# Decode attention with a token mixer: one 8 KB-row piece of the output weights loaded in five parts, x and a small bias through another queue

## The chip, the cores and the metric

The kernel runs on one core of a Trainium2 chip. The metric is the device time of one execution in microseconds (us): 1286.22 us is the median of three runs before the change (1286.08 to 1286.46). All data are float32.

## The reference, cut to what matters

One decode step over 8 sequences, with 32 query heads that share 8 key and value heads of 8192 cached positions, beside a token-mixing MLP:

```python
xn = layernorm(x)                                   # x: 8 x 1 x 512
# attention on layernorm'd xn
q  = (xn @ wq)                                      # 512 x 4096, 32 heads of 128
s  = einsum("bhqd,bhkd->bhqk", q, repeat(k_cache, 4)) * 128**-0.5
o  = einsum("bhqk,bhkd->bhqd", softmax(s), repeat(v_cache, 4))
A  = o.reshape(8, 1, 4096) @ wo                     # wo: 4096 x 512
# mixer over the token axis (one token, 1792 hidden units)
h  = layernorm(xn)
Bm = einsum("bdf,fs->bds", gelu(einsum("bsd,sf->bdf", h, w1) + b1), w2) + b2
out = x + A + transpose(Bm)
```

Each of the two caches holds 8 x 8 x 8192 x 128 numbers, 268 MB; wq and wo hold 8.4 MB each. Everything else is small.

## The kernel before, in words

The work is cut into 32 steps ("pairs"): one sequence and two of its key/value heads, whose keys (8.4 MB) and values (8.4 MB) lie in memory as 128 rows of 64 KB, one row for each partition. They go into a ring of five slots of 4 MB (`raw`). The loads of wq, of keys and values and of wo are all issued by the SyncE sequencer (SP in the profile, one queue, called q1 there), in the order in which the code calls `load` and `load_wo`; an issue waits until the slot that it writes has been read. Each load of 128 rows is divided over the core's 16 DMA engines, 8 rows each, and an engine works off the loads in the order of issue.

For each pair VectorE transposes the keys in 32x32 blocks (`turn`), TensorE makes the scores (`scores`), ScalarE the exponentials (`exps`), TensorE transposes them (`send_on`) and multiplies the values (`values`). Beside it ScalarE and GpSimd work through the mixer (`mx_step`). A loop (`tc.For_i`) runs over pairs 2 to 29 in twos; pairs 0 and 1, and 30 and 31, are written out. The order on each engine is the order of the code.

At the start x (8 rows of 2 KB) and b2 (one number, read into 8 partitions) are loaded through ScalarE's own queue (q10), and w1, b1 and w2 through GpSimd's (q0, whose descriptors GpSimd writes by software). x goes through the layer norm (`layer_norm`) and is turned into `lend`, the stationary operand of the q projection (`q_project`).

At the end wo, seen as 128 rows of 32 chunks of 512 numbers, comes in two halves (`load_wo`). The first half is one load of 128 rows of 32 KB. The second is cut by the table `WO_HIGH = (8, 4, 2, 1, 1)` into five loads of 16, 8, 4, 2 and 2 KB for each row, so that the last products wait for little: chunks 16 to 23, 24 to 27, 28 and 29, 30, 31. The matmuls of line 512 use chunks 0 to 27 (`sums`), ScalarE copies their result (`folded`), and `y_add` (line 520) adds chunks 28 to 31 and the folded sum in `hb`. VectorE copies the result (line 527) and SP stores it (line 528).

The framework gives each load that SP or ScalarE issues one of eight completion semaphores in turn (DMAHW0 to DMAHW7 in the listings of instructions), and each that GpSimd issues one of another set (DMASW0 and on). A load that is given a semaphore which an earlier load still has to raise is issued only after that load has landed.

Of the kernel before, what the change touches and what calls it, by code (L numbers as in the profile page):

```python
# [14 lines left out]
B, D, HQ, HKV, SK, DH, F = 8, 512, 32, 8, 8192, 128, 1792  # L15
REP = HQ // HKV
P = 128
# [22 lines left out]
ROUNDS = (LAST + 1 - 2 * FIRST) // PER  # L40
GROUPS = N_PR // PER
WO_HIGH = (8, 4, 2, 1, 1)
MJ = NF // PER
MIX = (4, 4)
PAD = 96
# [6 lines left out]
def attn_mixer_kernel(ctx: ExitStack, tc: tile.TileContext, x, kc, vc, wq, wo, w1, b1, w2, b2, out):  # L52
    nc = tc.nc
# [10 lines left out]
    def slot(at, n=1):  # L64
        return slots[:, at:at + n, :]
# [12 lines left out]
    def misc():  # L78
        return ps_m.tile([P, 512], F32, name="misc")
# [7 lines left out]
    RES = one.tile([HALF, NWO, ROUNDS], F32, name="res")  # L87
    lend = one.tile([P, 2, P], F32, name="lend")
    x_sb = OB[:B, 0, :]
    nc.scalar.dma_start(x_sb, x.rearrange("b s d -> (b s) d"))  # L90
    b2t = const.tile([B, 1], F32, name="b2t")
    nc.scalar.dma_start(b2t, bass.AP(tensor=b2.tensor, offset=b2.offset, ap=[[0, B], [1, 1]]))
    body = slot(2, 2).rearrange("p s m -> p (s m)")
    rows = wq.rearrange("(p e) n -> p (e n)", p=P)
    for a in range(2):
# [41 lines left out]
    def load_wo(high):  # L137
        t = slot(3 if high else 0).rearrange("p s (c n) -> p (s c) n", n=D)
        rows = wo.rearrange("(p c) n -> p c n", p=P)
        at = 0  # L140
        for n in WO_HIGH if high else (NWO // 2,):
            o = high * NWO // 2 + at
            nc.sync.dma_start(t[:, at:at + n], rows[:, o:o + n])  # L143
            for c in range(n):
                WO[o + c] = t[:, at + c]
            at += n
# [29 lines left out]
    m = misc()  # L176
# [16 lines left out]
    rows = tmp[:, :2 * REP]  # L193
# [7 lines left out]
    for k in range(2):  # L201
        for a in range(NB):
            o = a * W + a // 2 * HW
# [3 lines left out]
    for c in range(NCH):  # L207
        for s in range(2):
            o = s * HW + c * REP
# [17 lines left out]
    nc.gpsimd.memset(acc, 0.0)  # L227
    tabs = const.tile([P, ROUNDS, 2, MJ + 1], F32, name="tabs")
    tabw = const.tile([P, ROUNDS, MJ + 1], F32, name="tabw")
    for k in range(PER):  # L230
        js = slice(k * MJ, (k + 1) * MJ)
        for t, src in ((tabs[:, k::PER, 0], w1t), (tabs[:, k::PER, 1], b1t), (tabw[:, k::PER], w2t)):
            n = len(range(k, ROUNDS, PER))
            nc.gpsimd.tensor_copy(t[:, :, :MJ], src[:, js].unsqueeze(1).to_broadcast([P, n, MJ]))
    for t, src in ((tabs[:, :, 0], w1t), (tabs[:, :, 1], b1t), (tabw, w2t)):
        nc.gpsimd.tensor_copy(t[:, :, MJ:], src.unsqueeze(2))
    nows = const.tile([P, 2, MJ + 1], F32, name="nows")
    noww = const.tile([P, MJ + 1], F32, name="noww")
# [4 lines left out]
    for k in range(2):  # L243
        t = const.tile([P, CH_T * W + W], F32, name=f"pt{k}")
# [216 lines left out]
    with tc.For_i(0, ROUNDS, 1, iteration_sync=SYNC) as r:  # L461
        for k in range(PER):
            n = FIRST + k
# [18 lines left out]
    n = LAST - 1  # L482
# [11 lines left out]
    n = LAST  # L494
    score_half(n, True)
    load(vc, n, 2, 0)
    score_half(n, False)
    load(vc, n, 1, 1)
    load_wo(0)
    softmax_and_values(n, lambda: load_wo(1))  # L500
    take(n - 1)
    total(HALF)
# [7 lines left out]
    for c in range(FOLD):  # L510
        o = c % NB * W
# [44 lines left out]
```

## Time and profile before

| | |
|---|---|
| median of the runs | 1286.22 us (1286.08 to 1286.46) |
| the profiled execution | 1286.04 us |
| its span, first to last instruction | 1284.2 us |
| granted TensorE clock | 0.805 |
| TensorE busy | 767.5 us (60% of the span) |
| VectorE busy | 696.9 us (54%) |
| GpSimd / ScalarE busy | 248.1 us (19%) / 228.8 us (18%) |
| read from memory | 553.69 MB, 431 GB/s over the span |
| SP's DMA queue | 99.6% of the 16 DMA engines' time |

A row of a table by windows gives, for each stretch of the span, the busy time of each engine with its number of instructions, the granted clock, the share of the 16 DMA engines' time that packets took, and what they moved; a packet is counted where it starts, so a short window can show a share over 1. A row on a DMA queue gives its packets, their megabytes and their share of the 16 engines' time. In a row of the timeline stand start, length, engine, line, operation, and in brackets how long the engine was idle before it and what ended that.

### The profile page before, as it was taken

The numbers are of one execution on the slowest core, as the hardware profiler recorded it, in microseconds if no ns is written. First come the engines' busy times: TensorE is split into PE (matmuls) and PEld (weight loads), VectorE is DVE, ScalarE is ACT, GpSimd is POOL, SyncE is SP. The second block draws the span as 40 slices with busy tenths as digits, with TensorE's granted clock in tenths as the row PEclk, the third lists the DMA queues.
The fourth block names the chain that finished last, engine by engine and source line by source line (L and its number), as shares of the span: only waits on it lengthen the run. The fifth ranks groups of instructions, "written<-read, shape, count | busy, mean of one in ns | idle before, by whom it ended". The sixth has DMA issues, their size and how long they took to land. (4 is left out here: it accounts for less than half of the span.)

```text
span 1284.2 us, 13214 instructions
## 1 busy us (share of the span) xinstructions
PE 767.5 (60%) x4830; PEld 170.9 (13%) x4830; DVE 696.9 (54%) x615; ACT 228.8 (18%) x382; POOL 248.1 (19%) x244
## 2 busy tenths in 40 slices
PE   4367556576465665556666475765656665464677
PEld 1111111111011111111111011110111110011112
DVE  3666644466654465644466554565644466543661
ACT  0000221212222121221212222121221211222000
POOL 1000221202222022221212222022221212222000
PEclk8788787887777897788787777877778887778888
DMA  9999999999999999999999999999999999999998
GB/s 409 425 442 425 448 427 433 445 429 433 425 447 429 431 447 427 433 433 439 431 429 447 427 433 445 429 433 427 445 431 429 447 427 433 439 433 431 430 431 354
DMA packets 10975, 553.86 MB, mean 431 GB/s; under 512 B 1324, under 2 KB 1356, under 8 KB 1748
## 3 DMA queue, kind: packets, MB, share of 16 engines
q1 hardware_dynamic: 10836, 553.67, 99.6%
q8 instruction: 8, 0.13, 0.0%
q10 hardware_dynamic: 32, 0.02, 0.0%
q0 software_dynamic: 96, 0.02, 0.0%
q14 instruction: 3, 0.02, 0.0%
HBM read 553.69 MB, written 0.02 MB: 431 GB/s over the span
## 5 line engine op out<-in xcount | busy, mean ns | idle before, releaser
L293 DVE STREAM_TRANSPOSE raw<-raw 128x2048 f32<-128x2048 f32 x256 | 565.4, 2275 | 232.8 <-DMA raw<-in_A_k_cache_dram 218.6
L302 PE MATMUL acc<-raw,z 128*32 128x512 f32 x2048 | 372.8, 815 | 433.9 <-DVE raw L293 385.7
L340 PE MATMUL acc<-raw,pt 128*32 128x512 f32 x2048 | 245.5, 621 | 10.9 <-DMA raw<-in_A_v_cache_dram 5.5
L399 POOL TENSOR_TENSOR g<-g,noww 128x512 f32<-128x512 f32 x98 | 101.8, 1039 | 376.2 <-ACT g L394 376.2
L302 PEld LDWEIGHTS acc<-raw,z 128*32 128x32 f32 x2048 | 47.0, 124 | 737.7 <-DVE raw L293 550.9
L322 ACT ACTIVATE t2k<-acc,ns 128x512 f32<-128x512 f32 x32 | 22.0, 687 | 603.2 <-PE acc L340 525.5
L394 ACT ACTIVATE g<-hb,nows 128x512 f32<-128x512 f32 x112 | 87.5, 782 | 192.8 <-POOL macc L400 175.4
L329 DVE STREAM_TRANSPOSE pt<-misc 128x512 f32<-128x512 f32 x64 | 45.9, 717 | 126.0 <-PE misc L328 121.6
L397 POOL TENSOR_TENSOR macc<-g,noww 128x512 f32<-128x512 f32 x14 | 14.5, 1038 | 515.8 <-ACT g L394 515.8
L400 POOL TENSOR_TENSOR macc<-macc,g 128x512 f32<-128x512 f32 x84 | 106.4, 1267 | 6.6
L340 PEld LDWEIGHTS acc<-raw,pt 128*32 128x32 f32 x2048 | 66.0, 114 | 174.7 <-issue 150.0
L316 DVE TENSOR_TENSOR t2k<-misc,hmask 128x128 f32<-128x128 f32 x32 | 9.3, 292 | 114.8 <-PE misc L314 114.8
L328 PE MATMUL misc<-t2k,send 128*128 128x512 f32 x128 | 65.1, 632 | 3.1 <-ACT t2k L322 3.1
L394 ACT ACT_TABLE_LOAD x28 | 35.9, 1283 | 94.5 <-PE hb L385 94.3
L309 DVE TENSOR_REDUCE mr<-acc 128x1 f32<-128x512 f32 x32 | 22.1, 690 | 52.9 <-PE acc L302 52.9
L409 ACT ACT_TABLE_LOAD x28 | 35.9, 1283 | 0.5
L347 ACT COPY ob<-acc 128x512 f32<-128x512 f32 x32 | 18.7, 585 | 74.3 <-PE acc L340 74.3
L328 PEld LDWEIGHTS misc<-t2k,send 128*128 128x128 f32 x128 | 22.0, 191 | 45.2 <-issue 41.9
L405 PE MATMUL misc<-macc,esel 128*8 128x512 f32 x30 | 15.3, 590 | 19.6 <-DVE esel L403 19.6
L385 PE MATMUL hb<-hn,hsel 8*128 8x512 f32 x28 | 18.9, 761 | 12.9 <-DVE hsel L384 12.9
L406 DVE TENSOR_TENSOR yrow<-misc,yrow 8x512 f32<-8x512 f32 x16 | 10.9, 679 | 19.2 <-PE misc L405 19.2
L262 PE MATMUL misc<-raw,lend 128*32 128x512 f32 x64 | 12.5, 953 | 11.3 <-DMA raw<-in_A_wq_dram 11.3
(99 smaller groups left out, 195.4 us busy)
## 6 DMA issues: line engine op xcount, KB each, us to landing
raw<-in_A_v_cache_dram SPq DMA_DIRECT2D x4, 4096.0 KB, 34.3
raw<-in_A_wq_dram SPq DMA_DIRECT2D x2, 4096.0 KB, 17.0
raw<-in_A_k_cache_dram SPq DMA_DIRECT2D x2, 4096.0 KB, 30.8
raw<-in_A_wo_dram SPq DMA_DIRECT2D x1, 4096.0 KB, 26.4
raw<-in_A_wo_dram SPq DMA_DIRECT2D x1, 2048.0 KB
raw<-in_A_wo_dram SPq DMA_DIRECT2D x1, 1024.0 KB, 29.9
raw<-in_A_wo_dram SPq DMA_DIRECT2D x1, 512.0 KB
raw<-in_A_wo_dram SPq DMA_DIRECT2D x2, 256.0 KB, 30.8
```

What stands on the lines that cost most here:

```text
L293: nc.vector.transpose(t, t)
L302: nc.tensor.matmul(SD[n][c * W:(c + 1) * W, :].rearrange("p (t j) -> p t j", j=W), Z[:, n % PER, q, (1 - k) * REP:(1 - k) * REP + W], t[:, ...
L309: nc.vector.tensor_reduce(mr, SD[n], AX.X, ALU.max)
L322: nc.scalar.activation(p, SD.pop(n), AF.Exp, bias=ns, scale=SCALE, accum_out=lr[:, n % PER:n % PER + 1])
L328: nc.tensor.matmul(m, send[:, k, :], p, start=True, stop=True)
L329: nc.vector.transpose(PT[k][:, :CH_T * W], m)
L340: d = nc.tensor.matmul(OD[n][j * W:(j + 1) * W, :].rearrange("p (c d) -> p c d", c=NCH), PT[k][:, t * W:(t + 1) * W], v[:, t], start=(not ...
L385: nc.tensor.matmul(hb, hsel.to_broadcast([B, P]), hn, start=True, stop=True)
L394: nc.scalar.activation(g, hb7 if last else hb, AF.Gelu_apprx_tanh, bias=nows[:, 1, j:j + 1], scale=nows[:, 0, j:j + 1])
L399: nc.gpsimd.tensor_tensor(g, g, w, op=ALU.mult)
L400: nc.gpsimd.tensor_add(acc7 if last else acc, acc7 if last else acc, g)
L409: nc.scalar.activation(small.tile([P, 1], F32, name="warm"), nil, AF.Exp)
```

## The change

Two edits. x and b2 are issued by GpSimd in place of ScalarE. And the piece of the second half of wo that starts at chunk 24 (four chunks, 8 KB for each of 128 rows) is loaded by five loads of 112, 5, 5, 5 and 1 rows in place of one. All of it stays on SP's queue and in the same place of the program; the bytes are the same.

```diff
 WO_HIGH = (8, 4, 2, 1, 1)
+TILT_AT, TILT = 24, (112, 5, 5, 5, 1)
...
-    nc.scalar.dma_start(x_sb, x.rearrange("b s d -> (b s) d"))
+    nc.gpsimd.dma_start(x_sb, x.rearrange("b s d -> (b s) d"))
     b2t = const.tile([B, 1], F32, name="b2t")
-    nc.scalar.dma_start(b2t, bass.AP(tensor=b2.tensor, offset=b2.offset, ap=[[0, B], [1, 1]]))
+    nc.gpsimd.dma_start(b2t, bass.AP(tensor=b2.tensor, offset=b2.offset, ap=[[0, B], [1, 1]]))
...
             o = high * NWO // 2 + at
-            nc.sync.dma_start(t[:, at:at + n], rows[:, o:o + n])
+            p = 0
+            for m in TILT if o == TILT_AT else (P,):
+                nc.sync.dma_start(t[p:p + m, at:at + n], rows[p:p + m, o:o + n])
+                p += m
```

Lines behind the first edit have other numbers after the change: 143 becomes 146, 512 becomes 516, 520 becomes 524, 528 becomes 532.

The two edits act on one another through the semaphores. SP's queue at the end of the program before, from the last two value loads on; "128x2048" is the piece of 8 KB rows, the brackets name what an issue waits for:

```order
L122 DMA raw<-in_A_v_cache_dram 128x8192 [waits DVE_49]
L122 DMA raw<-in_A_v_cache_dram 128x8192 [waits DMAHW3_49,DVE_49,PE_49]
L143 DMA raw<-in_A_wo_dram 128x8192 [waits DVE_49,PE_49]
L143 DMA raw<-in_A_wo_dram 128x4096 [waits DMAHW4_49,PE_49]
L143 DMA raw<-in_A_wo_dram 128x2048
L143 DMA raw<-in_A_wo_dram 128x1024
L143 DMA raw<-in_A_wo_dram 128x512 x2
L528 DMA out_dram<-g 4x8x128 [waits DMAHW5_49,DVE_49]
```

The same place after the change:

```order
L123 DMA raw<-in_A_v_cache_dram 128x8192 [waits DVE_49]
L123 DMA raw<-in_A_v_cache_dram 128x8192 [waits DMAHW1_49,DVE_49,PE_49]
L146 DMA raw<-in_A_wo_dram 128x8192 [waits DVE_49,PE_49]
L146 DMA raw<-in_A_wo_dram 128x4096 [waits DMAHW2_49,PE_49]
L146 DMA raw<-in_A_wo_dram 112x2048
L146 DMA raw<-in_A_wo_dram 5x2048 x3
L146 DMA raw<-in_A_wo_dram 1x2048 [waits DMAHW3_49]
L146 DMA raw<-in_A_wo_dram 128x1024 [waits DMAHW4_49]
L146 DMA raw<-in_A_wo_dram 128x512 [waits DMAHW5_49]
L146 DMA raw<-in_A_wo_dram 128x512 [waits DMAHW6_49]
L532 DMA out_dram<-g 4x8x128 [waits DMAHW7_49,DVE_49]
```

One load became five, and the four loads of wo behind the three small ones now wait for a semaphore that an earlier load raises: DMAHW3 and DMAHW4 belong to the two halves of the last values, DMAHW5 to the first half of wo, DMAHW6 to its 16 KB-row piece.

TensorE's last matmuls before the change (line 512 with `sums`, line 520 with `hb`):

```order
L512 MATMUL acc<-raw,ot 32x512 [waits DMAHW0_49]
L512 MATMUL acc<-raw,ot 32x512 x7
L512 MATMUL acc<-raw,ot 32x512 [waits DMAHW1_49]
L512 MATMUL acc<-raw,ot 32x512 x3
L520 MATMUL hb<-raw,ot 32x128 [waits DMAHW2_49]
```

And after it:

```order
L516 MATMUL acc<-raw,ot 32x512 [waits DMAHW6_49]
L516 MATMUL acc<-raw,ot 32x512 x7
L516 MATMUL acc<-raw,ot 32x512 [waits DMAHW3_49,DMAHW2_49,DMAHW7_49,DMAHW1_49,DMAHW0_49]
L516 MATMUL acc<-raw,ot 32x512 x3
L524 MATMUL hb<-raw,ot 32x128 [waits DMAHW4_49]
```

The order is the same; the matmul that begins chunk 24 waits for five loads in place of one.

GpSimd's queue at the start, before:

```order
L552 UNCONDITIONAL_BRANCH [waits barrier_Pool_Activation_PE_DVE_SP_gather]
masks.py:197 MEMSET ident 128x128
masks.py:199 ISA
masks.py:199 AFFINE_SELECT ident<-ident 128x128 [waits Pool_49]
L156 DMA pad<-in_B_w_dram 128x14
```

And after:

```order
L556 UNCONDITIONAL_BRANCH [waits barrier_Pool_Activation_PE_DVE_SP_gather]
L91 DMA ob<-in_A_x_dram 8x512
L93 DMA b2t<-in_B_b_dram 8x1
masks.py:197 MEMSET ident 128x128
masks.py:199 ISA
masks.py:199 AFFINE_SELECT ident<-ident 128x128 [waits Pool_49]
L160 DMA pad<-in_B_w_dram 128x14
```

The two small loads now stand ahead of the identity matrix and of the loads of w1, b1 and w2, and ScalarE's queue has none left.

## The prediction

> **What bounds the kernel now.** I read the page's slices and DMA rows first, then the end of the chain of waits, then the last microseconds by windows, then the start by the timeline. The page:
>
> ```profile
> DMA  9999999999999999999999999999999999999998
> DMA packets 10975, 553.86 MB, mean 431 GB/s; under 512 B 1324, under 2 KB 1356, under 8 KB 1748
> q1 hardware_dynamic: 10836, 553.67, 99.6%
> q10 hardware_dynamic: 32, 0.02, 0.0%
> ```
>
> The 16 DMA engines are busy in every slice and SP's queue has 99.6% of their time. No compute engine is over 60%. So only three things can move the time: when the engines start, what they lose underway, and how evenly they end. 431 GB/s over 16 engines is 26.9 GB/s each, so one row of 8 KB takes an engine 8192 B / 26.9 GB/s = 0.304 us.
>
> The page also shows how a load is spread. x and b2 are two loads of 8 rows and have 32 packets on q10: 2 x (8 data + 8 completions), so each went to eight engines, a row each. By that a load of 5 rows goes to five engines, one of 1 row to one, and 112 rows give each of 16 engines 7.
>
> The end of the chain of waits (start, length, what), and SP's store behind it:
>
> ```profile
> 1249.57 30.87 DMA raw<-in_A_wo_dram
> 1280.44 0.04 issue
> 1280.48 0.47 PE hb L520 x8
> 1280.98 0.29 DVE g L527
> ...
> 1281.30 0.71 SPq L528 DMA_DIRECT2D out_dram<-g  x1
> ```
>
> The last piece of wo lands at 1280.44; what follows is fixed. The windows before it:
>
> ```profile
> 1277.50:1278.00 0.50, 0.38 (x8) 0.03 (x4) 0.00 (x0) 0.00 (x0) 0.00 (x0) 1.00 1.02 410
> 1278.25:1278.50 0.25, 0.25 (x8) 0.00 (x0) 0.00 (x0) 0.00 (x0) 0.00 (x0) 1.00 0.81 320
> ...
> 1279.50:1279.75 0.25, 0.25 (x17) 0.10 (x5) 0.00 (x0) 0.19 (x1) 0.00 (x0) 1.00 0.57 221
> 1279.75:1280.00 0.25, 0.25 (x16) 0.25 (x14) 0.00 (x0) 0.00 (x0) 0.00 (x0) 1.00 0.29 107
> 1280.00:1280.25 0.25, 0.25 (x16) 0.12 (x6) 0.00 (x0) 0.00 (x0) 0.00 (x0) 1.00 0.02 8
> ```
>
> The column before the last is the DMA share. Until 1278 all work; from 1278.25 some are done (0.81); from 1279.50 the share is 0.57 = 9 of 16 engines; these nine end between 1279.75 and about 1280.15 (0.4 us). The other seven end up to 1.8 us earlier. If all ended together, the gain would be at most 7 x 1.8 / 16 = 0.8 us: the most that any tilt of rows can bring.
>
> Why nine are late: DMA rows of the windows 40 to 160, 1195 to 1198 and 1190 to 1285 (fetches of instructions), then the packets from 1181.3 to 1182, 1182.7 to 1183.4 and 1279.6 to 1280.2.
>
> ```profile
> q8 instruction: 4, 0.07, 0.2%
> ...
> q8 instruction: 1, 0.02, 1.8%
> ...
> q8 instruction: 4, 0.07, 0.2%
> ```
>
> ```profile
> DMA packets 22, 0.72 MB, mean 1030 GB/s; under 512 B 11, under 2 KB 11, under 8 KB 11
> ...
> DMA packets 8, 0.26 MB, mean 375 GB/s; under 512 B 4, under 2 KB 4, under 8 KB 4
> ...
> DMA packets 38, 0.06 MB, mean 99 GB/s; under 512 B 9, under 2 KB 9, under 8 KB 38
> ```
>
> A fetch holds one engine for 1.8% x 16 x 3 us = 0.9 us. Packets under 512 B are the completion marks, one for each engine and load. In the loop's last rounds 11 marks come together and four about 1.4 us later, after four fetches; after four more, nine are late at the end. So the late ones are engines that fetched instructions, one each, and one more.
>
> Which engines those are no view says. But in the packet list each packet starts where the one before it on its engine ended, so the 16 sequences can be followed through, apart from a few that coincide in the first 12 us. Eight of them carry x's rows, that is, an 8-row load's engines. Whichever way the coinciding ones are taken, at least four of those eight end among the nine late ones.
>
> **The change part by part.**
>
> *The rows.* Before, each engine has 8 rows of the piece. After: 7 for all, one more on five engines three times, and one on a single engine. If the small loads take the same engines each time, and the single row one of these: one engine 11 rows (+3 x 0.304 = +0.91 us), four 10 (+0.61), eleven 7 (-0.30). If a 5-row load's engines are among the eight that an 8-row load uses, of which at most four are early, then at least one loaded engine is late already; and five drawn from all 16 with nine late would be all early with a chance of (7x6x5x4x3)/(16x15x14x13x12) = 0.5%. If it has +0.91, the end moves by 0.91 less what that engine is ahead of the last, 0 to 0.4: +0.5 to +0.9. If only engines with +0.61 are late: +0.2 to +0.6. Had none been late, the last engine would gain 0.30. Bounds -0.30 and +0.91; I take +0.6, since with half of the eight late the odds are even for the one with eleven rows, and the latest counts.
>
> *TensorE.* Chunks 24 to 27 wait for the slowest of five loads, by the same sum +0.3 to +0.9 late:
>
> ```profile
> 1275.55 0.13 PEld L512 LDWEIGHTS acc<-raw,ot 128*32 128x32 f32 x4 [0.32 <-DMA raw<-in_A_wo_dram]
> 1277.97 0.16 PEld L512 LDWEIGHTS acc<-raw,ot 128*32 128x32 f32 x8 [1.03 <-DMA raw<-in_A_wo_dram]
> ...
> 1280.48 0.16 PEld L520 LDWEIGHTS hb<-raw,ot 128*32 128x32 f32 x8 [0.36 <-DMA raw<-in_A_wo_dram]
> ```
>
> The last wait (0.36 us of idle left) moves by as much as the first, so this costs 0; should chunk 24 slip more than the last piece, what exceeds 0.36 would come on top.
>
> *SP.* Four issues more, 2.31 / 5 = 0.46 us each, 1.8 us, and four new waits in a row. Behind the waiting sequencer stand only the pieces of 4, 2 and 2 KB and the store.
>
> ```profile
> 1247.70 2.31 SPq L143 DMA_DIRECT2D raw<-in_A_wo_dram  x5
> 1253.85 0.62 PE L340 MATMUL acc<-raw,pt 128*32 128x512 f32 x2
> 1261.14 5.12 PE L340 MATMUL acc<-raw,pt 128*32 128x512 f32 x32 [2.29 <-DMA raw<-in_A_v_cache_dram]
> 1270.80 8.24 PE L512 MATMUL acc<-raw,ot 128*32 128x512 f32 x56 [2.72 <-DMA raw<-in_A_wo_dram]
> 1282.30:1282.60 0.30, 0.00 (x0) 0.00 (x0) 0.00 (x0) 0.00 (x0) 0.00 (x0) 1.00 0.00 0
> 1282.60:1282.70 0.10, 0.00 (x0) 0.00 (x0) 0.00 (x0) 0.00 (x0) 0.00 (x0) 1.00 0.22 61
> ```
>
> The loads waited for have landed by 1253.85, 1261.1, 1270.8 and, for the last issue, 1275.55 (the 16 KB-row piece). From issue to first packet the store took 1282.6 - 1281.3 = 1.3 us, so the last piece is ready at about 1276.9. A late engine, with eight rows of 2 KB (8 x 0.076 = 0.6 us) left, wants it at 1279.5 or so; the earliest ones at about 1278.3 - 0.6 - 0.3 = 1277.4. Cost 0, with 0.5 us to spare there and over 2 us where it counts. Bounds: 0 and whatever the issue lags beyond 2.6 us.
>
> *x and b2.* Rows of the start, with the DMA row of the first 3 us and, for GpSimd's three loads, the time from issue to landing:
>
> ```profile
> q10 hardware_dynamic: 16, 0.02, 4.0%
> ...
> DMA to landing us min/median/max: 7.8/9.6/10.5
> 0.74 0.59 ACTq L90 DMA_DIRECT2D ob<-in_A_x_dram  x1
> 1.48 0.70 POOL L156 DMA_DIRECT2D pad<-in_B_w_dram  x1 [0.16 <-issue]
> 2.18 0.54 POOL L157 DMA_DIRECT2D pad<-in_B_b_dram  x1
> 2.69 0.68 DVE L163 BATCH_NORM_STATS2 st<-ob 8x6 f32<-8x512 f32 x1 [1.80 <-DMA ob<-in_A_x_dram]
> ...
> 5.46 0.19 DVE L179 COPY lend<-misc 128x32 f32<-128x32 f32 x1 [0.66 <-PE misc L178]
> 13.40 6.06 PE L262 MATMUL misc<-raw,lend 128*32 128x512 f32 x32 [7.98 <-DMA raw<-in_A_wq_dram]
> 22.80 6.47 PE L262 MATMUL misc<-raw,lend 128*32 128x512 f32 x32 [3.34 <-DMA raw<-in_A_wq_dram]
> 32.44 8.89 DVE L293 STREAM_TRANSPOSE raw<-raw 128x2048 f32<-128x2048 f32 x4 [17.87 <-DMA raw<-in_A_k_cache_dram]
> 43.92 0.52 POOL L418 MEMSET rep<- 128x512 f32 x1 [29.01 <-POOLq L461]
> ```
>
> GpSimd's loads took 7.8 to 10.5 us to land, so x lands at worst at 0.75 + 10.5 = 11.3, in place of 2.69. `lend` then is ready 2.96 us later, at 14.2, and the q projection starts 0.8 us late; its second half waits for wq until 22.80, with 3.34 us of idle before it: covered. VectorE's constants slip by up to 8.6 us into its 17.87 us of idle; GpSimd issues two more (1.25 us) into 29.01. Only if x came after 14 would SP's next key load be touched. For the DMA engines it is the same bytes: x's eight engines lose its share ahead of wq, 4.0% x 16 x 3 us / 8 = 0.24 us, and later serve them between wq's packets. Bounds -0.24 and +0.1; I take 0, since these engines are not behind at the end of it.
>
> Sum: 1286.04 + 0.6 = 1286.64 against the profiled execution. That lies 0.18 under the median, so 1286.8 for the runs.
>
> **The rivals.**
>
> 1. *The loaded engines are early ones:* -0.30, so 1285.9. For it: seven engines have 0.4 us or more to spare. Against: the count above, four late of eight; the fetches would have to fall on other engines after the change. 0.2.
> 2. *The change does not tilt:* 5 + 5 + 5 + 1 = 16, and if each small load took the next engines in turn, every engine would have 8 rows as before: 1286.2. No row shows whether two small loads share engines. 0.1. The Trainium skill's page DMA: Bandwidth & Descriptors, "Why a DMA increments its semaphore by 16 and not by 1", says that a load issued by SP uses the lowest-numbered engines; by that the rows pile up, as I took it.
> 3. *Engines get in each other's way:* in a load of 128 rows an engine always writes the same partitions; with 112 rows, 7 each, and rows 112 to 127 by other engines, their ways into memory may cross. Two that share a way would take 0.61 for a row; if that holds for half of an engine's 8 rows it is +1.2: 1287.4. For it: each engine runs at just the same rate now, which sharing would break. Against: no row shows sharing. 0.14. The skill's page SBUF — State Buffer, "Door 1: The DMA port swizzle", has such a rule: 16 ports, each for fixed groups of partitions, whose number reached sets the rate. By it the 112 rows don't divide evenly.
> 4. *The other side, slower beyond doubt:* SP's last wait becomes the bound. It decides once issue to first packet takes more than some 4 us in place of 1.3; for +2.6 us it must take 6.6: 1288.8. The queue's other first packets speak against it. 0.04.
>
> **How the numbers follow.** The forecast has 0.5, the rivals 0.2, 0.1, 0.14 and 0.04, something unseen 0.02. This kernel's time can be told from no change at about 0.2%, 2.6 us. Forecast and rivals 1 to 3 lie within it; rival 4 and a part of 3 don't: faster 0.02, same 0.92, slower 0.06. Range: from rival 1 with x's 0.24 (1285.7) to rival 3 (1287.4) with 0.3 on top, 1285.7 to 1287.7.
>
> **What would show it.** After the change, the share in the last windows should fall from 16 engines to nine as now, but one to five engines should end 0.3 to 0.9 us behind; the last wait of line 524 should end at about 1281.0. SP should issue wo in four bursts, the last at about 1275.6. The first layer norm should start at 6 to 11 us, and the q projection's second half still at 22.8. If the last wait ends at 1280.1 it is rival 1; if the piece of 8 KB rows takes clearly over 3 us, rival 3. Wrong altogether would be a gap in the DMA share at 1276 to 1279, or other engines fetching instructions.

## The result, and the profile after

The change costs 4.6 us: 1290.69 us (median of seven runs, 1289.29 to 1291.49) against 1286.08 (1285.69 to 1286.49) for the kernel before in the same call. The ratio is 1.0034 [1.0022, 1.0046]: slower by more than 0.2%, and outside the predicted range. The profiled execution took 1290.96 us with a span of 1289.2 us (before 1284.2), so 5.0 us are to be found in it.

The page and the DMA queues after the change:

```profile
DMA packets 11023, 553.86 MB, mean 430 GB/s; under 512 B 1372, under 2 KB 1404, under 8 KB 1796
q1 hardware_dynamic: 10852, 553.67, 99.5%
```

The bytes are those of before. SP's queue has 16 packets more (10836 before): the completion marks of 5 + 5 + 5 + 1 engines, so the small loads do go to five, five, five and one engine. DMA is still the bound. But look at what it moves at the end, by windows (the last two columns are the DMA share and GB/s), after:

```profile
1275.00:1276.00 1.00, 1.00 (x12) 0.32 (x8) 0.00 (x0) 0.00 (x0) 0.00 (x0) 0.83 1.02 229
1276.00:1277.00 1.00, 0.87 (x10) 0.00 (x0) 0.00 (x0) 0.00 (x0) 0.00 (x0) 1.00 1.03 238
...
1278.00:1279.00 1.00, 1.00 (x12) 0.26 (x8) 0.00 (x0) 0.00 (x0) 0.00 (x0) 1.00 1.13 205
...
1281.00:1282.00 1.00, 0.00 (x0) 0.00 (x0) 0.00 (x0) 0.00 (x0) 0.00 (x0) 1.00 0.99 330
1282.00:1283.00 1.00, 0.88 (x8) 0.23 (x8) 0.00 (x0) 0.00 (x0) 0.00 (x0) 0.58 0.59 225
...
1283.50:1283.75 0.25, 0.25 (x4) 0.00 (x0) 0.00 (x0) 0.00 (x0) 0.00 (x0) 0.50 0.07 25
```

and before:

```profile
1275.00:1276.00 1.00, 1.00 (x16) 0.35 (x12) 0.00 (x0) 0.00 (x0) 0.00 (x0) 1.00 1.04 438
1276.00:1277.00 1.00, 1.00 (x16) 0.40 (x12) 0.00 (x0) 0.00 (x0) 0.00 (x0) 1.00 1.00 418
```

The share is about 1 in both, so no engine waits for work. After the change the same 16 busy engines move half as much. A busy share tells that packets are under way, not how fast. The queue's rows give the size of it; before, from 1276 to 1278:

```profile
DMA packets 210, 0.80 MB, mean 398 GB/s; under 512 B 23, under 2 KB 23, under 8 KB 173
...
q1 hardware_dynamic: 210, 0.80, 97.1%
```

After, from 1276 to 1280:

```profile
DMA packets 159, 0.83 MB, mean 206 GB/s; under 512 B 29, under 2 KB 29, under 8 KB 87
...
q1 hardware_dynamic: 159, 0.83, 98.0%
```

For 8192 B that is 0.971 x 16 x 2 us / 0.80 MB x 8192 B = 0.32 us of an engine before, and 0.980 x 16 x 4 / 0.83 x 8192 = 0.62 after. (These rows mix the piece with its neighbours.) Taken one by one in the packet list, the piece's rows took 0.309 us each before and 0.54 in the mean after (up to 0.80; the first fifteen or so still 0.309). The loads beside the piece, which are not cut, stretch too: 16 KB rows from 0.61 to as much as 1.15, 4 KB rows from 0.16 to as much as 0.44 (0.27 in the mean). For one engine the means add up to 8 x (0.54 - 0.31) = 1.8 us more in the piece, 0.9 in its eight rows of 4 KB and 0.3 in the rows of 16 and 2 KB, 3.0 us together. The data end at 1283.74 where before it was 1280.13.

The end of the chain of waits, and SP's store:

```profile
1250.23 31.70 DMA raw<-in_A_wo_dram
1281.92 0.20 issue
1282.12 1.93 PE acc L516 x8
1284.06 1.99 PE hb L524 x40
...
1286.38 0.66 SPq L532 DMA_DIRECT2D out_dram<-g  x1
```

The last link is no longer the last load with eight matmuls behind it, but chunk 24's wait, which ends at 1282.12 (1277.97 before) with TensorE's whole rest of the program behind it. So the store's issue, 5.08 us later than the 1281.30 of before, is made of 3.6 us of later data and some 1.5 us of TensorE: from the end of the data to the store it was 1281.30 - 1280.13 = 1.17 before and 1286.38 - 1283.74 = 2.64 now.

Not all of the 3.6 us belongs to the piece. The first key load behind the loop was issued 1.05 us later than before; SP's row and the window from 1180 to 1240, before and then after:

```profile
1198.67 0.34 SPq L122 DMA_DIRECT2D raw<-in_A_k_cache_dram  x1
1180.00:1240.00 60.00, 33.85 (x203) 6.71 (x203) 38.80 (x30) 4.54 (x8) 5.65 (x5) 0.78 1.00 430
```

```profile
1199.72 0.34 SPq L123 DMA_DIRECT2D raw<-in_A_k_cache_dram  x1
1180.00:1240.00 60.00, 33.29 (x203) 6.70 (x203) 37.81 (x30) 4.54 (x8) 6.48 (x6) 0.77 0.99 426
```

4 GB/s less over 60 us are 0.24 MB, some 0.6 us at 430 GB/s. This lies ahead of wo's loads, and the kernels below have it or not without a pattern that I can name. About 3 us remain for the piece and the rows that it slows, as the sum over the rows gave.

### The profile page after: what moved, and what is told of

Read it like the earlier page. It is cut to its first block, busy times and chain, and to the rows that moved or that the text cites. A ratio compares the mean times of both kernels' runs of the same rounds, so it can differ in the third digit from the quotient of the medians.

```text
span 1289.2 us, 13234 instructions
## 1 busy us (share of the span) xinstructions
PE 766.1 (59%) x4830; PEld 171.4 (13%) x4830; DVE 696.8 (54%) x615; ACT 228.7 (18%) x382; POOL 248.6 (19%) x246
## 5 line engine op out<-in xcount | busy, mean ns | idle before, releaser
L365 PE MATMUL misc<-ob,pick 128*32 128x128 f32 x256 | 18.1, 276 | 0.8 <-ACT ob L351 0.8
```

## The experiments

All start from the changed kernel. The median of the kernel before was 1286.05 to 1286.20 in these calls.

**x and b2 alone.** The piece is one load again.

```diff
-TILT_AT, TILT = 24, (112, 5, 5, 5, 1)
+TILT_AT, TILT = 24, (P,)
```

> x and b2 on GpSimd's queue, the piece of 8 KB rows as one load. Theory A (in the load of 112 rows the DMA engines write and read out of their usual groups of rows and slow each other: 8 KB packets took about 0.56 us in place of 0.31 after the change): 1286.1, within 0.5 of before; the wo pieces run at 420 to 440 GB/s to 1278, the first key load after the loop may be issued 1 us late or not. Rival X (the late x costs, by shifting the work at the start and so the first issue after the loop, 1199.7 in place of 1198.7): 1286.8 to 1287.5 with that issue at 1199.5 or later.

1286.48 us (1286.05 to 1287.63, ten runs), ratio 1.0004 [0.9994, 1.0013]. The rate at the end is the old one:

```profile
1274.00:1276.00 2.00, 0.89 (x12) 0.26 (x12) 0.00 (x0) 0.00 (x0) 0.00 (x0) 1.00 0.96 408
```

The rate is whole, so the loss is not in this edit; of its +0.4 us the interval cannot tell whether it is more than nothing.

**The rows alone.** x and b2 go back to ScalarE.

```diff
-    nc.gpsimd.dma_start(x_sb, ...
+    nc.scalar.dma_start(x_sb, ...
-    nc.gpsimd.dma_start(b2t, ...
+    nc.scalar.dma_start(b2t, ...
```

> The piece in loads of 112, 5, 5, 5 and 1 rows, x and b2 on ScalarE's queue as before. Theory A: the whole loss or nearly, 1289.5 to 1291, with 200 to 250 GB/s at a DMA share near 1 for 4 to 5 us after the 16 KB-row piece. Rival X: 1.0 us less than the changed kernel, since x is not late. If both edits were needed together it is 1286.1.

1291.38 us (1290.46 to 1291.54, five runs), ratio 1.0039 [1.0024, 1.0053].

```profile
1274.00:1276.00 2.00, 0.80 (x8) 0.00 (x0) 0.00 (x0) 0.00 (x0) 0.00 (x0) 1.00 0.97 242
1276.00:1278.00 2.00, 0.57 (x4) 0.16 (x8) 0.00 (x0) 0.00 (x0) 0.00 (x0) 0.92 1.00 217
```

The whole loss is the cut's, some 0.4 us over the top of theory A's range.

**Five loads, cut by columns.** Each of the five loads covers all 128 rows; their number, their semaphores and SP's four waits are the same.

```diff
-TILT_AT, TILT = 24, (112, 5, 5, 5, 1)
+TILT_AT, TILT = 24, (512, 512, 512, 256, 256)
...
-                nc.sync.dma_start(t[p:p + m, at:at + n], rows[p:p + m, o:o + n])
+                nc.sync.dma_start(to[:, p:p + m], src[:, p:p + m])
```

> x on GpSimd's queue; the piece again in five loads, at the same place and with the same four waits of SP for semaphores, but each of all 128 rows and of a part of the columns (512, 512, 512, 256, 256 of the 2048 numbers of a row). Theory A: 1286.1 to 1286.9 (its packets of 2 and 1 KB cost some 0.3 us more than those of 8 KB). Rival W (SP's waits for semaphores, or five completions in place of one, hold up the end): as the changed kernel, 1290 to 1291. Rival T (tilt: engines with more rows end late) does not apply here, so also 1286.1.

1286.19 us (1285.87 to 1286.82, ten runs), ratio 1.0000 [0.9990, 1.0009], with the old rate:

```profile
1274.00:1276.00 2.00, 0.86 (x12) 0.16 (x8) 0.00 (x0) 0.00 (x0) 0.00 (x0) 1.00 1.00 388
1276.00:1278.00 2.00, 2.00 (x21) 0.63 (x14) 0.00 (x0) 0.00 (x0) 0.00 (x0) 1.00 1.05 406
```

So it is neither the waits of SP, nor five completions in place of one, nor more and smaller packets. It is the cut by rows.

**A cut without a tilt.** Two loads; 16 rows go to 16 engines, one each, so every engine has eight rows as before.

```diff
-TILT_AT, TILT = 24, (112, 5, 5, 5, 1)
+TILT_AT, TILT = 24, (112, 16)
```

> x on GpSimd's queue; the piece in two loads of 112 and 16 rows: every engine has 7 + 1 = 8 rows as before, so nothing is tilted, and SP's waits for the values and the first half of wo are nearly gone. Theory A: 1289 to 1291, since the 112 rows still fall out of the usual groups; packets of 8 KB at 0.5 us and more. Rival T (the tilt of up to 3 rows on five engines makes the loss): 1286.1. Rival W (waits): 1286.1 to 1286.5.

1289.68 us (1289.24 to 1291.29, seven runs), ratio 1.0030 [1.0019, 1.0042]. The window of the piece, that of the last matmuls, and the end of the chain:

```profile
1276.00:1278.00 2.00, 2.00 (x20) 0.51 (x16) 0.00 (x0) 0.00 (x0) 0.00 (x0) 0.83 1.00 238
...
1282.00:1284.00 2.00, 1.89 (x44) 0.80 (x40) 0.00 (x0) 0.58 (x1) 0.00 (x0) 1.00 0.34 129
...
1281.70 1.11 PE acc L516 x8
...
1282.83 0.59 ACT t2k L518
...
1283.47 0.95 PE hb L524 x24
...
1284.44 0.29 DVE g L531
```

Evenly loaded engines run at half rate as well. What the tilt itself adds is not resolved: the intervals of this kernel and of the change overlap. In its profiled execution (1289.55 us) the first key load behind the loop was as early as before (1198.67), so those +3.5 us have nothing of that in them.

**Another source.** As the last one, but the piece is read from rows that lie 8 KB apart in memory in place of 64 KB; the products of chunks 24 to 27 so use other weights.

```diff
+            src = rows[:, o:o + n]
+            if o == TILT_AT:
+                src = wo.rearrange("(q p c) n -> q p c n", p=P, c=n)[o // n]
```

> As the kernel with loads of 112 and 16 rows, but the piece is read from other places of wo: rows that lie one behind the other (8 KB apart in memory, not 64 KB), into the same partitions, so the wrong weights are used for chunks 24 to 27. Theory A1 (the engines meet where they write into the partitions): as with 112 and 16 rows, 1289 to 1291, packets of 8 KB at 0.5 us and more. Rival A2 (they meet where they read: rows 64 KB apart, 7 rows an engine, fall on the same part of memory): 1286.1 to 1286.5, packets at 0.31 us.

1290.14 us (1289.16 to 1290.91, eight runs), ratio 1.0030 [1.0019, 1.0041].

```profile
1276.00:1278.00 2.00, 0.00 (x0) 0.00 (x0) 0.00 (x0) 0.00 (x0) 0.00 (x0) 1.00 0.98 236
```

Rows 8 KB apart lose as much as rows 64 KB apart, so it is not the distance at which they are read.

**Halves, and sixteens.** `TILT = (64, 64)`, and in another kernel `(16, 16, 16, 16, 64)`.

> The piece in two loads of 64 rows: 4 + 4 rows for each engine, no tilt. Theory A1 in the form of 16 ways into the partitions, each for two groups of four rows 32 apart: 64 rows in a row reach 8 of them, so two engines share each and an 8 KB packet takes 2 x 0.309 = 0.62 us; the piece takes 4.9 in place of 2.5 us, and with the packets of other loads that it holds up 1288.5 to 1290.5. Rival A3 (only counts of rows that don't divide evenly, such as 7 an engine, are slow): 1286.1 to 1286.5 at 0.31 us.

> The piece in loads of 16, 16, 16, 16 and 64 rows, one row an engine in the first four. Theory A1 in the form of 16 ways: 16 rows in a row reach 4 of them, so up to four engines share one: packets of up to 4 x 0.309 = 1.2 us in the first half of the piece and 0.6 in the second; 1290 to 1293, slower than with 64 and 64 rows. Rival A4 (sharing halves the rate whatever the rows): packets of 0.6 us, as 64 and 64 rows.

1291.01 us (1289.74 to 1291.58, five runs), ratio 1.0036 [1.0022, 1.0050], and 1290.35 us (1289.11 to 1291.08, seven runs), ratio 1.0033 [1.0022, 1.0044]. The halves, then the sixteens:

```profile
1276.00:1278.00 2.00, 1.15 (x12) 0.16 (x8) 0.00 (x0) 0.00 (x0) 0.00 (x0) 1.00 0.97 233
```

```profile
1276.00:1278.00 2.00, 1.11 (x8) 0.40 (x12) 0.00 (x0) 0.00 (x0) 0.00 (x0) 0.74 0.99 238
```

Both at the same half rate, with 8 KB packets of 0.547 and 0.525 us in the mean; the halves came out 0.5 us over the top of their range, and the sixteens not slower than the halves, against what was expected of them. The Trainium skill's page SBUF — State Buffer, "Door 1: The DMA port swizzle (why `[64,N]` ≈ `[32,N]`)", sets the rate by the number of 16 ports that the partitions reach. Partitions 0 to 63 reach eight of them by it, and so do 64 to 127: half the rate, and the halves agree. Sixteen in a row, such as 0 to 15, reach four, a quarter of it, by an estimate packets of 4 x 0.309 = 1.2 us; the longest here was 0.76.

That estimate puts all 16 engines into one load of 16 rows at the same time, and the trace shows that they were not: the completion marks of the first such load landed for seven engines between 1274.37 and 1274.67 and for the other nine between 1276.54 and 1277.51. Seven engines on four ports would take 7 / 4 x 0.309 = 0.54 us for a packet, again an estimate. So the expectation of 1.2 us falls, and the rule behind it is neither refuted nor shown by this run. What the runs show by themselves is a rate about halved, whatever the cut by rows.

**Twice the piece, a quarter of it.** The cut moves to the 2 MB piece at chunk 16, `TILT_AT, TILT = 16, (112, 16)`, and to the last 256 KB, `31, (64, 64)`.

> The cut into 112 and 16 rows at the 16 KB-row piece in place of the 8 KB-row piece: twice the bytes out of their groups, none tilted. Theory A: packets of 16 KB at 1.0 to 1.2 us in place of 0.61, and about twice the loss of the 8 KB-row piece, less what TensorE has to spare there: 1290 to 1294. If the loss comes from the end alone (pieces late in the program waited for one by one) and not from the bytes: 1288 to 1290.

> x on GpSimd's queue; the piece of 8 KB rows in one load, and the last piece (128 rows of 2 KB, a quarter of the bytes) in two loads of 64 rows. Theory A (rows out of their groups cost about the time of their bytes once more to twice more): the 0.65 us of this piece become 1.3 to 2, so 1286.6 to 1287.5, packets of 2 KB in it at 0.15 us and more. If the loss is a fixed cost of a load that is cut (4 us whatever its size): 1290. If the other engines' lag hides it: 1286.2.

1295.52 us (1295.30 to 1295.74, two runs), ratio 1.0072 [1.0052, 1.0092]; and 1286.60 us (1286.42 to 1287.87, eleven runs), ratio 1.0005 [0.9996, 1.0014]. Rate of the former from 1270 to 1280, and the end of the latter's chain:

```profile
1270.00:1280.00 10.00, 6.26 (x32) 1.59 (x32) 0.00 (x0) 0.00 (x0) 0.00 (x0) 0.66 0.97 205
```

```profile
1279.76 0.59 ACT t2k L518
...
1280.40 1.05 PE hb L524 x24
...
1281.47 0.29 DVE g L531
```

The loss grows with the bytes that are cut: +9.3 us for 2 MB (its 16 KB packets took 1.16 us in the mean), +3.6 to +5.3 for 1 MB, and for 256 KB nothing beyond the 0.4 that the x edit's kernel shows as well. The +9.3 lies over the range of 1290 to 1294; a part of it is TensorE, whose last 24 matmuls of line 516 ran for 5.35 us at a clock of 0.50. The end of the data leaves TensorE out: against 1280.13 before it moved by 7.2 us for 2 MB, by 3.0 to 4.4 for the cuts of 1 MB and by 0.3 for 256 KB, in one profiled execution of each, some with the late key load in them. The times of the last dose cannot tell it from nothing, but its packets do: 53 of the last 256 rows of 2 KB took longer than the usual 0.084 us, up to 0.26.

**One engine with more rows.** The piece is whole; ahead of it one row of 32 KB of values is loaded into a slot that is read no more, 1.2 us of work for a single engine.

```diff
+            if o == TILT_AT:
+                nc.sync.dma_start(slots[:1, 4, :], pairs[id(vc)][0].rearrange("(p m) -> p m", p=P)[:1, :SIZE])
```

> x on GpSimd's queue, the piece in one load; ahead of it one more load of a single row of 32 KB (of the values, into a slot that is free), which nobody uses: one engine gets 1.21 us of extra work, in a single packet, and little is written out of its group. It tries the prediction's sum for the tilt by itself. If the engine that a one-row load uses is one of the nine late ones: the end moves by 0.8 to 1.2 us, 1286.9 to 1287.6, and the last wait for wo ends at about 1281.1 to 1281.6. If it is one of the early ones (1.4 to 1.8 us ahead): nothing, 1286.0 to 1286.5.

1286.63 us (1286.29 to 1287.32, eleven runs), ratio 1.0004 [0.9995, 1.0013], 0.15 above x and b2 alone. Its last wait ended at 1281.08, but its first key load behind the loop was late too (1199.39), which explains as much. In the packet list that engine had been 1.15 us ahead of the last one: it began the extra row at 1274.58, and the last engine ended its 16 KB rows at 1275.73. The time falls between the two ranges that were expected. So a load of one row takes an engine with time to spare, and a tilt on it costs next to nothing; for the engines of a 5-row load this was not tried.

No version was faster than the kernel before; the cut by columns and x and b2 alone equal it within their intervals.

## Why the prediction was wrong, point by point

*The rows: the step that failed.* The sum priced a row of the piece at the 0.304 us of the whole queue and asked only how many rows an engine has. A row took 0.54 us in the mean after the cut, and 0.52 to 0.56 in the other kernels whose piece of 1 MB is cut by rows, tilt or none. That is the mechanism of rival 3, engines in each other's way, which had 0.14 and was sized at +1.2 for half of an engine's eight rows; it measured about +3 on the data's end, because nearly all rows were slow (+1.8 for an engine's eight) and the rows of the loads beside them as well (+1.2). By the prediction's own sign, a piece that takes clearly over 3 us, it is rival 3: eight rows of 0.54 are 4.3 us. The row cited against it, that no row shows sharing, was empty: before the change every large load covered all 128 rows, so sharing could not show. An absent price should have widened the range, by the rival's own mechanism applied to all eight rows (8 x 0.3 = +2.4) and to the neighbours.

The Trainium skill's page DMA: Bandwidth & Descriptors, "Rules for kernel authors", says of two transfers to disjoint partition halves not to bother and to use one transfer of 128 partitions. The trace agrees and puts a loss on it: +4.8 us for the halves of 1 MB.

*TensorE costs 0: failed, by some 1.5 us.* The step held only if chunk 24 slipped no more than the last piece plus 0.36 us. Chunk 24's wait slipped by 4.15 us and the end of the data by 3.6, so by that condition 0.2 us come on top. The larger part is a term that the step did not have: the matmuls behind the wait ran under a clock of 0.50 (windows above), where it was 1.00 before:

```profile
1282.12 1.93 PE L516 MATMUL acc<-raw,ot 128*32 128x512 f32 x8 [2.44 <-DMA raw<-in_A_wo_dram]
1284.11 0.58 ACT L518 COPY t2k<-acc 128x512 f32<-128x512 f32 x1 [16.32 <-PE acc L516]
```

From chunk 24's wait to VectorE's copy it took 1286.07 - 1282.12 = 3.95 us here. In the kernel with 112 and 16 rows the same matmuls ran at a clock of 1.00 and took 1284.44 - 1281.70 = 2.74 us. So the clock made some 1.2 us of this profile; why it stood at 0.50 was not tried, and it does not come with the cut, which the kernel with 112 and 16 rows has too.

*SP's four waits cost 0: right*, shown by the cut by columns. The last issue came at 1277.73 in place of the predicted 1275.6, since the 16 KB-row piece that it waits for was itself slowed, and the DMA share still has no gap behind it:

```profile
1277.73 0.33 SPq L146 DMA_DIRECT2D raw<-in_A_wo_dram  x1
...
1280.00:1281.00 1.00, 0.00 (x0) 0.00 (x0) 0.00 (x0) 0.00 (x0) 0.00 (x0) 1.00 0.95 252
```

*x and b2 cost 0: right*, as far as the interval of their run alone can tell. x landed inside the bounds of 6 to 11 us, and the q projection's second half still waits for wq, 0.3 us later than before:

```profile
8.09 0.68 DVE L167 BATCH_NORM_STATS2 st<-ob 8x6 f32<-8x512 f32 x1 [7.19 <-DMA ob<-in_A_x_dram]
...
23.12 5.07 PE L266 MATMUL misc<-raw,lend 128*32 128x512 f32 x32 [3.16 <-DMA raw<-in_A_wq_dram]
```

*The tilt of +0.6: not shown, and its engine wrongly chosen.* The size is below the spread of the cut kernels. But the completion marks in the traces tell who was late: the load of one row, on the engine with eleven rows by the step's own account, had landed at 1280.59 and the last of the five loads at 1281.92; with the rows alone it was 1280.52 and 1282.22. So that engine was 1.3 to 1.7 us ahead, as in the one-row kernel, where the step gave it even odds of being late. The last to land was a load of five rows, 0.36 us behind the 112 rows; what the extra rows of its engine cost cannot be told apart here.

*Not foreseen at all:* the first key load behind the loop, some +0.6 us in this profile. It was 1198.6 to 1198.8 in the profiles of x and b2 alone, the columns, 112 + 16, the sixteens and the last piece, and 1199.2 to 1199.8 in the other five experiments. Its cause was not tried.

What remains argued and not shown is where engines meet. On the reading side one other placement of the rows lost as much; the cut by columns keeps each load at all 128 partitions and loses nothing. That points to the writing side. One more sign fits it: the last completion mark of the piece landed 0.31 to 0.36 us after the end of its last row before the change, in the cut by columns and in the kernels that leave the piece whole, and 0.80 to 0.90 us after it in all six kernels that cut the piece of 8 KB rows by rows. But no run shows the part of the memory for which the engines queue, nor why 112 + 16 rows lose as much as 64 + 64.

## What to carry to other kernels

A load that fills all 128 partitions is better cut by columns than by rows: the former was free here, the latter halved the rate of 16 busy engines for the piece and for the loads around it. Read GB/s beside the DMA share, since a share of 1 hides a halved rate. And where a transfer near the end may slip, follow the chain of compute behind it: the slip first uses up the idle time in that chain, and what is left of the chain can run at a lower clock than it had in the profile before.

## What the runs showed of the hardware

- Cuts into 112 and 16, 64 and 64, or 16, 16, 16, 16 and 64 of 128 rows run at about the same rate, 233 to 238 GB/s from 1276 to 1278, against 406 for a cut by columns.
- The slowing spreads to whole loads in flight beside the cut one: 16 KB packets from 0.61 to as much as 1.15 us, 4 KB packets from 0.16 to 0.27 in the mean.
- The last completion mark of a piece cut by rows landed 0.80 to 0.90 us after the end of its last row, against 0.31 to 0.36 for one that is whole or cut by columns.
- GpSimd's load of x took 6.8 us from issue to landing beside SP's full queue, by the profile's list of loads; ScalarE's took some 1.95 (issued at 0.74, landed by 2.69).
